# Splits without GpSimd, softmax sums under one reciprocal, and logits computed as rows, in a fused attention, mixture-of-experts and feed-forward kernel

## The chip, the cores and the metric

One core of one Trainium2 chip. The engines are TensorE (PE; its weight loads are shown as PEld), VectorE (DVE), ScalarE (ACT), GpSimd (POOL) and SyncE (SP, which here issues DMAs); each works through its own queue in order. The metric is the device time of one execution in microseconds.

## The reference

Attention over q, k, v of shape (4, 8, 576, 64) is a sum of two softmax attentions: one on rows averaged in fours (144 x 144 scores per head, the result repeated four times), and one on a band |i - j| < 4.

```python
out_up = np.repeat(sm_attn(q_d, k_d, v_d), 4, axis=2)       # q_d, k_d, v_d: means of four rows
scores = np.where(np.abs(pos[:, None] - pos[None, :]) < 4, scale * q @ k.T, -1e9)
x = (out_up + softmax(scores) @ v)                            # -> (2304, 512)
```

Then a mixture of 8 experts with a skip: only tokens with `x @ w_skip > 0` are computed, each by the expert with the largest logit, `x + p * (relu(x @ w1[e]) @ w2[e])`, with w1 (8, 512, 1024) and w2 (8, 1024, 512). Last a feed-forward: `h = x @ w_in` (512 to 2048), `g = h * sigmoid(1.702 h)`, `g @ w_out`.

## The kernel before

Matrix products of the experts and of the feed-forward run in float16 with split operands: a tensor t is scaled by a power of two, `high = f16(t)`, `low = f16(t - high)`, and three products (high high, high low, low high) are summed in PSUM. So each operand needs a maximum or a sum of squares (for the power of two), a high part and a low part. `pow2_into` and `pow2_scale` make the powers on DVE from exponent bits.

**Attention (`phase_a`)**: 16 units of two heads. Each step is a small function with a due time in `STAGE_A`; steps of all units are sorted by unit number plus due time and issued in that order; only SP's queue is then tied to that order, the rest is left to a scheduler that keeps it by priority. Of a unit: `ldq`, `ldv`, `ldw` load (SP), `qd`, `kd` sum rows in fours (DVE), `pd`, `pl`, `pk` are the scores (PE), `md` the maxima of the averaged scores and their scaling (DVE, L375, L376), `ed` the exponentials with their sums (ACT, L383), `mk`, `ml`, `sb`, `el` the same for the band, `rl` (L407 to L409) and `rd` (L414, L415) the reciprocals of the sums, `nl`, `nd` the products with them (POOL), `pq`, `pp` transposes, `pdt`, `pt` copies (ACT), `po`, `pn`, `pm` the products with v, `xt` the sum of both (DVE), `xm` its absolute maximum (DVE, L499), `px`, `xn` transpose and store. After every second unit `lg` (L530) forms 9 logits (8 experts and skip) for 576 tokens with the 9 logits on partitions; `le` (L539, L541) adds them up, and once per batch `tl` (L547) transposes them to tokens on partitions and `la` (L552) copies them for the routing (`route0` and on). PSUM has three double buffers (`big`) and two single ones (`small`). Steps of `Win` prepare w_in beside it.

**Experts (`phase_b`)**: each expert has 192 slots. `STAGE_B` gives due times again, and here all engines' queues are tied to that order. For an expert: `gather`, `xprep` (PE transposes), `xh`, `xl` (split of x), `l1` in four parts (PE, into PSUM `ph`, four buffers), `l1e` (ACT, relu to float32 `ht`, two buffers, L820), `l1h` (DVE, cast to `hh`, L823), `l1l` (POOL, `hl = ht - hh`, L827), `l2` in four parts (PE, L839, L846), `yrow`, `ymx`, `yadd`, `scatter`. The next experts' weights are loaded (`load`), squared and summed (`bound`, ACT, L689), scaled (`scale`, `scb`) and split (`hi` on ACT, L715, or DVE, L717; `lo` on DVE, `wl`, L723).

**Feed-forward (`phase_c`)**: 6 blocks of 384 tokens; layer one of a block is 16 column tiles `f` of 12 matmuls each (L1097, PSUM `ph`, three buffers), layer two runs two blocks behind (L1117). After each tile: sigmoid on ACT (L1101), the product `sg = ph * gs * sg` on DVE (L1102), and one tile later, in `late`, the cast `gh` on ACT (L1089) and the low part `gl` (L1090), on POOL in blocks 0 to 2 and on DVE after. `Wout` prepares w_out beside the first 40 tiles: load, `w64a` (ACT), `w64l`, `w64f` (DVE, L130 to L132), square (ACT, L231), scale, `woh` (ACT), `wol` (DVE, L243).

Of the kernel before, what the change touches and what calls it, by code (L numbers as in the profile page):

```python
# [80 lines left out]
def pow2_scale(nc, pool, m, name, squared=False):
# [19 lines left out]
    l10=-2.8750, l1e0=-2.5414, l1h0=-2.1815, l1l0=-2.0258, l20=-1.6661, l11=-2.8473, l1e1=-2.5379, l1h1=-2.2714,  # L101
    l1l1=-1.8902, l21=-1.5453, l12=-2.1639, l1e2=-1.9897, l1h2=-1.8716, l1l2=-1.8041, l22=-1.3442, l13=-2.0520,
    l1e3=-1.8744, l1h3=-1.8562, l1l3=-1.7262, l23=-1.2374, scale=-2.2810, scb=-2.1764, bound00=-3.9127,
    hi00=-3.1600, lo00=-2.9149, load00=-2.9138, bound01=-3.5859, hi01=-2.6890, lo01=-2.5881, load01=-2.5870,
    bound10=-2.7781, hi10=-2.1111, lo10=-1.8915, load10=-1.8904, bound11=-2.5563,
    hi11=-1.7296, lo11=-1.6624, load11=-1.6613, gather=-4.7500, xprep=-3.9203, xh=-3.5055, xl=-2.9872,
    giv=-1.1000, yrow0=-1.0047, yrow1=-1.0040, ymx=-0.8644, yadd0=-0.6966, scatter0=-0.6711,
# [1171 lines left out]
```

## Time and profile before

| | us |
|---|---|
| median of 3 runs | 803.38 |
| lowest, highest | 798.86, 803.81 |
| the profiled execution | 801.5 |
| its span, first to last instruction | 799.7 |

The span begins with attention (to about 200 us), then the experts (to about 391 us), then the feed-forward. The profile gives busy time by engine: PE 694.6 us, DVE 478.1, ACT 394.0, POOL 297.7; the mean granted TensorE clock is 0.948 of full speed. A busy PE is modelled, as its matmuls are pipelined: it says that PE has work in flight, not that it is at its peak. The views used below are the table of busy time by stretch, the groups of instructions by line, the list of who waited for whom, one line's spread of durations, and instructions in order of time.

### The profile page before, as it was taken

What the parts mean: (1) busy time and instruction counts of PE and PEld (TensorE: products, weight loads), DVE (VectorE), ACT (ScalarE), POOL (GpSimd) and SP (SyncE); (2) the same over time, 40 slices, a digit from 0 to 9 for tenths busy, and PEclk for the clock granted to TensorE, in tenths of its full rate; (3) what the DMA queues carried; (4) which work ended last, traced back from release to release, by engine and by line L of the source; (5) the groups of instructions that cost most, each with busy time, mean ns of one, the idle gap of its engine ahead of it and who ended that gap; (6) DMA issues with size and microseconds to landing.
All of it is one profiled execution on the core that took longest, in us unless ns stands there. A gap on an engine that the chain in (4) does not pass through costs nothing.

```text
span 799.7 us, 15485 instructions
## 1 busy us (share of the span) xinstructions
PE 694.6 (87%) x6207; PEld 430.8 (54%) x6207; DVE 478.1 (60%) x909; ACT 394.0 (49%) x806; POOL 297.7 (37%) x294
## 2 busy tenths in 40 slices
PE   4478978878499899878499899999999999999997
PEld 3355655655376666655265555545545545544443
DVE  8889997996588888899468996204503511520000
ACT  1566665763687667763167876414413412421111
POOL 8555644650346999987334444300000000000000
PEclk9977997999599999999799999999999999999999
DMA  9956998617456666520344331001000000000000
GB/s 259 263 152 174 301 285 260 158 33 258 113 205 237 241 234 240 189 73 16 119 132 146 123 102 27 1 26 54 1 27 14 1 13 27 1 14 27 27 27 27
DMA packets 43007, 92.49 MB, mean 116 GB/s; under 512 B 10398, under 2 KB 24354, under 8 KB 38837
## 3 DMA queue, kind: packets, MB, share of 16 engines
q1 hardware_dynamic: 25908, 81.11, 31.6%
q10 hardware_dynamic: 14208, 4.87, 2.6%
q0 software_dynamic: 2816, 5.50, 2.4%
q8 instruction: 50, 0.82, 0.4%
q14 instruction: 25, 0.20, 0.1%
HBM read 79.55 MB, written 12.92 MB: 116 GB/s over the span
## 4 chain that ended last, share of the span: by engine, by line
PE 48%; DVE 19%; POOL 11%; issue 9%; DMA 8%; ACT 4%; SPq 1%; POOLq 0%; ACTq 0%; DVEq 0%
PE po L1117 22%; PE ph L1097 17%; DMA w64r<-in_moe_w_in 5%; POOL hl L827 3%; DVE wl L723 3%; POOL g L881 3%; DVE w64l L131 2%; POOL ids L911 2%; POOL g L768 2%; DVE sg L1102 2%; DVE w64f L132 1%; DVE wol L243 1%; PE po L464 1%; DVE w64l L130 1%; DMA vw<-in_vwin 1%
## 5 line engine op out<-in xcount | busy, mean ns | idle before, releaser
L1102 DVE SCALAR_TENSOR_TENSOR sg<-ph,gs,sg 128x384 f32<-128x384 f32 x96 | 58.7, 615 | 132.3 <-ACT sg L1101 132.1
L1097 PEld LDWEIGHTS <-wih 128*128 128x128 f16 x768 | 76.2, 100 | 60.1 <-issue 12.4
L1123 ACT ACTIVATE o<-po,os 128x128 f32<-128x128 f32 x72 | 20.5, 367 | 148.8 <-PE po L1117 93.4
L1117 PEld LDWEIGHTS <-gh 128*128 128x128 f16 x576 | 56.3, 98 | 66.0
L1097 PE MATMUL ph<-xh,wih 128*128 128x384 f16 x384 | 79.5, 330 | 8.4 <-DVE sg L1102 7.5
L723 DVE SCALAR_TENSOR_TENSOR wl<-raw,w_s,wh 128x2048 f16<-128x2048 f32 x32 | 81.3, 2574 | 4.4 <-ACT wh L715 2.9
L1097 PE MATMUL ph<-xh,wil 128*128 128x384 f16 x384 | 79.9, 330 | 0.0
L1090 POOL TENSOR_TENSOR gl<-sg,gh 128x384 f16<-128x384 f32 x48 | 49.2, 1027 | 81.7 <-ACT gh L1089 63.2
L1097 PE MATMUL ph<-xl,wih 128*128 128x384 f16 x384 | 78.9, 328 | 0.0
L1089 ACT CAST gh<-sg 128x384 f16<-128x384 f32 x96 | 48.8, 509 | 47.8 <-DVE sg L1102 47.6
L1101 ACT ACTIVATE sg<-ph,ih 128x384 f32<-128x384 f32 x96 | 55.4, 578 | 33.2 <-PE ph L1097 31.1
L1117 PE MATMUL po<-woh,gh 128*128 128x512 f16 x288 | 67.1, 379 | 0.0
L689 ACT ACTIVATE jk<-raw 128x2048 f16<-128x2048 f32 x32 | 61.1, 1908 | 9.3 <-DVE mx L686 8.7
L1117 PE MATMUL po<-wol,gh 128*128 128x512 f16 x288 | 65.3, 379 | 0.0
L1117 PE MATMUL po<-woh,gl 128*128 128x512 f16 x288 | 65.1, 379 | 0.0
L827 POOL TENSOR_TENSOR hl<-ht,hh 128x384 f16<-128x384 f32 x32 | 43.5, 1372 | 27.2 <-DVE hh L823 17.4
L1097 PEld LDWEIGHTS <-wil 128*128 128x128 f16 x384 | 38.0, 99 | 25.5 <-issue 1.2
L812 PEld LDWEIGHTS <-wh 128*128 128x128 f16 x512 | 44.1, 101 | 4.4 <-ACT wh L715 2.3
L1117 PEld LDWEIGHTS <-gl 128*128 128x128 f16 x288 | 28.2, 98 | 34.0
L715 ACT ACTIVATE wh<-raw,w_s 128x2048 f16<-128x2048 f32 x16 | 31.3, 1995 | 29.6 <-DVE w_s L77 18.2
L1090 DVE TENSOR_TENSOR gl<-sg,gh 128x384 f16<-128x384 f32 x48 | 26.8, 558 | 26.5 <-ACT gh L1089 26.5
L812 PE MATMUL ph<-xh,wl 128*128 128x192 f16 x256 | 32.7, 252 | 3.9 <-DVE wl L723 3.6
(228 smaller groups left out, 1343.5 us busy)
## 6 DMA issues: line engine op xcount, KB each, us to landing
raw<-in_moe_w SPq DMA_DIRECT2D x32, 1024.0 KB
w64r<-in_moe_w_in SPq DMA_DIRECT2D x16, 512.0 KB
w64r<-in_moe_w_out SPq DMA_DIRECT2D x16, 512.0 KB
vw<-in_vwin SPq DMA_DIRECT2D x32, 216.0 KB
qt<-in_q SPq DMA_DIRECT2D x16, 288.0 KB
kt<-in_k SPq DMA_DIRECT2D x16, 288.0 KB
vn<-in_v SPq DMA_DIRECT2D x16, 288.0 KB
xd<-xn ACTq DMA_DIRECT2D x16, 288.0 KB
```

Of the source, the lines that this page charges most:

```text
L689: self.nc.scalar.activation(j, r, AF.Square, accum_out=self.mx[i][:, hf, wi:wi + 1])
L715: self.nc.scalar.activation(t, r, AF.Copy, scale=s)
L723: self.nc.vector.scalar_tensor_tensor(t, r, s, self.h[e, wi, hf], op0=ALU.mult, op1=ALU.subtract)
L812: T.matmul(ph[:, fi, :], wa[:, k_, o:o + P], xa[:, k_, :], start=(n == 0), stop=(n == 3 * NK - 1))
L827: G.tensor_tensor(hl[:, 2 * fp:2 * fp + 2, :], hr.pop((e, fp)), hh[:, 2 * fp:2 * fp + 2, :], ALU.subtract)
L881: G.tensor_tensor(g, g, yr[e][:, cols(ti)].rearrange("p (h w) -> p h w", w=DM // 2), ALU.add)
L1089: A.copy(split[1], split[0])
L1090: (nc.gpsimd if b <= ahead else V).tensor_tensor(split[2], split[0], split[1], ALU.subtract)
L1097: T.matmul(ph, wa[:, k_, f * P:(f + 1) * P], xx[:, k_, :], start=(n == 0), stop=(n == 3 * NK - 1))
L1101: A.activation(sg, ph, AF.Sigmoid, scale=ih[:, f:f + 1])
L1102: V.scalar_tensor_tensor(sg, ph, gs[:, f:f + 1], sg, op0=ALU.mult, op1=ALU.mult)
L1117: T.matmul(po, ga[:, f, i * P:(i + 1) * P], wa[:, f, :], start=(n == 0), stop=(n == 3 * (DF // P) - 1))
```

## The change

In attention `md` no longer scales; the scaling is a small ACT copy in `ed`. The sums of both softmaxes lie in one tile (13 columns, three tiles in turn), so `rl` takes one reciprocal for both and `rd` goes; the factor 4 that `rd` had goes into the copy `pdt`. `xm` is a sum of squares on ACT, and the scale of x comes from a bound by it. `lg` takes x as the stationary operand and the 9 gate columns as the moving one, so that logits come out with tokens on partitions; `tl` and `la` go. For the experts `l1e` goes: ACT writes `hh` from PSUM, and DVE computes `hl` from PSUM with a max and a subtraction; the due times of the old `l1e` and `l1h` are now those of `l1h` and `l1l`. In the feed-forward one gelu activation replaces sigmoid and product; `gh` and `gl` take the scale.

```diff
@@ pow2_into, pow2_scale: a target exponent t instead of 15 @@
+XT, WT = 3, 8
...
@@ STAGE_B @@
-    l10=-2.8750, l1e0=-2.5414, l1h0=-2.1815, l1l0=-2.0258, l20=-1.6661, ...
+    l10=-2.8750, l1h0=-2.5414, l1l0=-2.1815, l20=-1.6661, ...
...
@@ phase_a @@
+    sums = [cst.tile([P, NTL + 4], F32, name=f"sums{i}") for i in range(3)]
...
     def md(u):
-        V.tensor_scalar(m, m, -0.125 / 16.0, None, op0=ALU.mult)
...
     def ed(u):
-        d["rd"] = r = sm.tile([NPL, 4], F32, tag="rd", name="rd")
+        r = sums[u % 3][:NPL, NTL:NTL + 4]
+        mb = sm.tile([NPL, 4], F32, tag="mb", name="mb")
+        A.activation(mb, d["md"], AF.Copy, scale=-0.125 / 16.0)
...
     def rl(u):
-        d["rl"] = r = sm.tile([P, NTL], F32, tag="rl", name="rl")
-        V.tensor_reduce(r, d["sl"], axis=AX.X, op=ALU.add)
+        r = sums[u % 3]
+        V.tensor_reduce(r[:, 0:NTL], d["sl"], axis=AX.X, op=ALU.add)
         V.tensor_scalar(r, r, 1.0e-9, None, op0=ALU.add)
         V.reciprocal(r, r)
-    def rd(u):
-        r = units[u]["rd"]
-        V.tensor_scalar(r, r, 1.0e-9, 4.0, op0=ALU.add, op1=ALU.mult)
-        V.reciprocal(r, r)
...
     def pdt(u):
-        A.copy(o, d["pq"][:NPL, :, 0:4 * NPL])
+        A.activation(o, d["pq"][:NPL, :, 0:4 * NPL], AF.Copy, scale=0.25)
...
     def xm(u):
-        V.tensor_reduce(c["xm"][:, u:u + 1], units[u]["xt"], axis=AX.X, op=ALU.max, apply_absolute_value=True)
+        j = wk.tile([P, S], F16, tag="xj", name="xj", bufs=1)
+        A.activation(j, units[u]["xt"], AF.Square, accum_out=c["xm"][:, u:u + 1])
...
     def lg(u):
-        o = units[u]["lg"] = big("lg")
-        for a in range(2):
+        o = units[u]["lg"] = small("lg")
+        for j in range(NTB):
             for i in range(2):
-                T.matmul(o[:9, a, 0:S // 2], wg9[:, units[u - 1 + i]["pr"], :],
-                         units[u - 1 + i]["xt"][:, a * S // 2:(a + 1) * S // 2], start=(i == 0), stop=(i == 1))
+                T.matmul(o[:TB, 9 * j:9 * j + 9], units[u - 1 + i]["xt"][:, TB * j:TB * (j + 1)],
+                         wg9[:, units[u - 1 + i]["pr"], :], start=(i == 0), stop=(i == 1))
...
     def le(u):
-        src = d["lg"][:9, :, 0:S // 2]
+        src = d["lg"][:TB, 0:9 * NTB].rearrange("p (j e) -> p j e", j=NTB)
...
-    def tl(b):
...
-    def la(b):
...
@@ Experts.scale2: one operation less for iv @@
...
@@ phase_b @@
-    V.tensor_copy(c["xmax"], mp)
-    sx, ix = pow2_scale(nc, c["cp"], c["xmax"], "sx")
+    sx, ix = pow2_scale(nc, c["cp"], mp, "sx", True, t=XT)
+    V.tensor_scalar(c["xmax"], ix, 2.0 ** XT, None, op0=ALU.mult)
...
-    def l1e(e, fp):
-        ph, (hh, hl) = phs.pop((e, fp)), hts[e]
-        hr[e, fp] = t = wk.tile([P, 2, CAP], F32, tag="ht", name="ht")
-        A.activation(t, ph, AF.Relu, scale=C20)
     def l1h(e, fp):
-        V.tensor_copy(hts[e][0][:, 2 * fp:2 * fp + 2, :], hr[e, fp])
+        A.activation(hts[e][0][:, 2 * fp:2 * fp + 2, :], phs[e, fp], AF.Relu)
     def l1l(e, fp):
-        hh, hl = hts[e]
-        G.tensor_tensor(hl[:, 2 * fp:2 * fp + 2, :], hr.pop((e, fp)), hh[:, 2 * fp:2 * fp + 2, :], ALU.subtract)
+        hh, hl = (h[:, 2 * fp:2 * fp + 2, :] for h in hts[e])
+        V.scalar_tensor_tensor(hl, phs.pop((e, fp)), 0.0, hh, op0=ALU.max, op1=ALU.subtract)
...
@@ phase_c @@
-    gs = sm.tile([P, NF], F32, name="gs")
-    V.tensor_scalar(gs, win.si, smin, C20, op0=ALU.mult, op1=ALU.mult)
+    gs = sm.tile([P, 1], F32, name="gs")
+    V.tensor_scalar(gs, sx, smin, C20, op0=ALU.mult, op1=ALU.mult)
...
         def late():
             if split:
-                A.copy(split[1], split[0])
-                (nc.gpsimd if b <= ahead else V).tensor_tensor(split[2], split[0], split[1], ALU.subtract)
+                A.activation(split[1], split[0], AF.Copy, scale=gs)
+                V.scalar_tensor_tensor(split[2], split[0], gs, split[1], op0=ALU.mult, op1=ALU.subtract)
...
-            A.activation(sg, ph, AF.Sigmoid, scale=ih[:, f:f + 1])
-            V.scalar_tensor_tensor(sg, ph, gs[:, f:f + 1], sg, op0=ALU.mult, op1=ALU.mult)
+            A.activation(sg, ph, AF.Gelu_apprx_sigmoid, scale=ih[:, f:f + 1])
```

## Rows read from the trace of the kernel before

**Rows 1.** Busy us (x instructions) of PE, PEld, DVE, ACT, POOL; PE clock, DMA share, GB/s.

```profile
40.00:120.00 80.00, 64.27 (x1086) 46.69 (x1084) 73.79 (x181) 51.56 (x156) 42.96 (x47) 0.85 0.79 228
...
240.00:340.00 100.00, 90.88 (x893) 65.87 (x890) 88.34 (x109) 70.79 (x80) 85.34 (x60) 0.98 0.65 228
...
400.00:480.00 80.00, 73.22 (x458) 45.92 (x457) 68.72 (x114) 59.49 (x126) 32.32 (x30) 0.98 0.38 125
480.00:800.00 320.00, 314.36 (x1650) 162.34 (x1649) 78.09 (x137) 99.26 (x218) 16.84 (x18) 0.99 0.06 20
```

**Rows 2.** DVE by line, 0 to 200: busy us, mean ns | idle before, releaser.

```profile
L499 DVE TENSOR_REDUCE xm<-xt 128x1 f32<-128x576 f32 x16 | 11.8, 738 | 0.1
...
L414 DVE TENSOR_SCALAR rd<-rd 72x4 f32<-72x4 f32 x16 | 5.8, 365 | 4.0 <-ACT sd L383 3.1 <-POOL vd L328 0.8
...
L376 DVE TENSOR_SCALAR md<-md 72x4 f32<-72x4 f32 x16 | 3.1, 192 | 0.0
...
L541 DVE TENSOR_TENSOR le<-le,lg 9x576 f32<-9x576 f32 x4 | 2.9, 737 | 0.9 <-PE lg L530 0.9
...
L415 DVE RECIPROCAL rd<-rd 72x4 f32<-72x4 f32 x16 | 2.6, 161 | 0.1
```

**Rows 3.** PE in order of time, end of attention: start, us, line, records.

```profile
184.81 2.11 PE L530 MATMUL lg<-xt,wg 128*9 128x288 f32 x8
...
187.63 1.27 PE L464 MATMUL po<-pt,vw 128*64 128x64 f32 x36
...
193.60 0.45 PE L547 MATMUL tl<-ident,le 9*96 9x9 f32 x6
```

**Rows 4.** ACT by line, 0 to 200: a square with a sum.

```profile
L181 ACT ACTIVATE w64j<-w64f 128x512 f16<-128x512 f32 x16 | 10.0, 628 | 8.2 <-DVE w64f L132 6.8 <-DVE md L376 0.9 <-DVE rd L415 0.4
...
L181 ACT ACTIVATION_READ_ACCUMULATOR w64j<-w64f 128x1 f32 x16 | 3.0, 188 | 0.0
```

**Rows 5.** SP's DMA issues in order of time: two band windows, eight units apart.

```profile
51.37 0.84 SPq L320 DMA_DIRECT2D vw<-in_vwin  x2
...
131.53 1.04 SPq L320 DMA_DIRECT2D vw<-in_vwin  x2
```

**Rows 6.** Experts, 240 to 340: cast and subtraction by line, the cast's min/median/max.

```profile
L823 DVE CAST hh<-ht 128x384 f16<-128x384 f32 x20 | 11.8, 611 | 10.1 <-ACT ht L820 10.1
...
L827 POOL TENSOR_TENSOR hl<-ht,hh 128x384 f16<-128x384 f32 x21 | 31.6, 1513 | 6.8 <-DVE hh L823 6.6
...
L823 DVE CAST hh<-ht x20: 346/396/1420, 242.2 to 338.1; 128x384 f16<-128x384 f32 x20
```

**Rows 7.** Who waited for whom, 190 to 400: us, times, longest.

```profile
PE py L839 <- DVE wl L723: 15.4, 7, 4.3
...
ACT ht L820 <- POOL hl L827: 13.8, 5, 3.2
```

**Rows 8.** PE in order of time: layer two begins for experts 1, 2, 6.

```profile
253.87 0.59 PE L839 MATMUL py<-wh,hh 128*128 128x512 f16 x2
...
272.32 0.59 PE L839 MATMUL py<-wh,hh 128*128 128x512 f16 x2
...
358.72 0.59 PE L839 MATMUL py<-wh,hh 128*128 128x512 f16 x2
```

**Rows 9.** Feed-forward: a wait (399 to 481), min/median/max of lines, groups by line.

```profile
PE ph L1097 <- DVE sg L1102: 7.5, 8, 2.2
...
L1102 DVE SCALAR_TENSOR_TENSOR sg<-ph,gs,sg x96: 601/618/620, 406.4 to 707.1; 128x384 f32<-128x384 f32 x96
...
L1101 ACT ACTIVATE sg<-ph,ih x96: 560/580/592, 405.8 to 706.5; 128x384 f32<-128x384 f32 x96
...
L1089 ACT CAST gh<-sg x96: 493/511/529, 407.1 to 707.8; 128x384 f16<-128x384 f32 x96
...
L243 DVE SCALAR_TENSOR_TENSOR wol<-w64f,wo_s,woh 128x512 f16<-128x512 f32 x11 | 12.0, 1102 | 0.0
...
L243 DVE SCALAR_TENSOR_TENSOR wol<-w64f,wo_s,woh x16: 740/752/1404, 436.3 to 498.5; 128x512 f16<-128x512 f32 x16
...
L1101 ACT ACT_TABLE_LOAD x1 | 1.3, 1283 | 0.0
```

More of the change, by code (lines that the diff above doesn't have):

```diff
@@ L76, in pow2_into, with pow2_scale @@
     V.tensor_scalar(e, e, 64.0 * ONE, 200.0 * ONE, op0=ALU.max, op1=ALU.min)
-    V.tensor_scalar(s.bitcast(I32), e, -1.0, 268.0 * ONE, op0=ALU.mult, op1=ALU.add)
-    V.tensor_scalar(si.bitcast(I32), e, 14.0 * ONE, None, op0=ALU.subtract)
-def pow2_scale(nc, pool, m, name, squared=False):
+    V.tensor_scalar(s.bitcast(I32), e, -1.0, (253.0 + t) * ONE, op0=ALU.mult, op1=ALU.add)
+    V.tensor_scalar(si.bitcast(I32), e, (t - 1.0) * ONE, None, op0=ALU.subtract)
+def pow2_scale(nc, pool, m, name, squared=False, t=15):
     e = pool.tile([P, 1], I32, name=f"{name}_e")
@@ L100 @@
 STAGE_B = dict(
[L101 to L107, printed above, removed]
+    l10=-2.8750, l1h0=-2.5414, l1l0=-2.1815, l20=-1.6661, l11=-2.8473, l1h1=-2.5379, l1l1=-2.2714, l21=-1.5453,
+    l12=-2.1639, l1h2=-1.9897, l1l2=-1.8716, l22=-1.3442, l13=-2.0520, l1h3=-1.8744, l1l3=-1.8562, l23=-1.2374,
+    scale=-2.2810, scb=-2.1764, bound00=-3.9127, hi00=-3.1600, lo00=-2.9149, load00=-2.9138, bound01=-3.5859,
+    hi01=-2.6890, lo01=-2.5881, load01=-2.5870, bound10=-2.7781, hi10=-2.1111, lo10=-1.8915, load10=-1.8904,
+    bound11=-2.5563, hi11=-1.7296, lo11=-1.6624, load11=-1.6613, gather=-4.7500, xprep=-3.9203, xh=-3.5055,
+    xl=-2.9872, giv=-1.1000, yrow0=-1.0047, yrow1=-1.0040, ymx=-0.8644, yadd0=-0.6966, scatter0=-0.6711,
     yadd1=-0.6113, scatter1=-0.6009, scat0=-2.8208, scat1=-2.5500, scat2=-1.6433)
@@ L294, in phase_a @@
     vws = [cst.tile([P, NTL, 2, D], F32, name=f"vw{i}") for i in range(4)]
+    sums = [cst.tile([P, NTL + 4], F32, name=f"sums{i}") for i in range(3)]
+    for t in sums:
+        V.memset(t, 1.0)
     for t in vws:
@@ L418, in nd @@
         d = units[u]
[L419 removed]
+        G.tensor_tensor(d["sd"], d["sd"], sums[u % 3][:NPL, NTL:NTL + 4, None].to_broadcast([NPL, 4, 2 * NPL]), ALU.mult)
     def nl(u):
         d = units[u]
[L423 removed]
+        G.tensor_tensor(d["sl"], d["sl"], sums[u % 3][:, 0:NTL, None].to_broadcast([P, NTL, KW]), ALU.mult)
     def pq(u):
@@ L535, in le @@
         r = rt[d["b"]]
-        src = d["lg"][:9, :, 0:S // 2]
+        src = d["lg"][:TB, 0:9 * NTB].rearrange("p (j e) -> p j e", j=NTB)
         if d["pr"] == 1:
-            r["le"] = sm.tile([9, 2, S // 2], F32, tag="le", name="le", bufs=2)
-            V.tensor_copy(r["le"], src)
-        else:
-            V.tensor_tensor(r["le"], r["le"], src, ALU.add)
-    def tl(b):
-        rt[b]["tl"] = o = small("tl")
-        le = rt[b]["le"].rearrange("e a t -> e (a t)")
-        for j in range(NTB):
-            T.transpose(o[:TB, 9 * j:9 * j + 9], le[:, TB * j:TB * (j + 1)], ident[:9, :9])
-    def la(b):
-        r = rt[b]
-        r["l"] = sm.tile([TB, NTB, 9], F32, tag="l", name="l", bufs=2)
-        V.tensor_copy(r["l"], r["tl"][:TB, 0:9 * NTB].rearrange("p (j e) -> p j e", j=NTB))
+            r["l"] = sm.tile([TB, NTB, 9], F32, tag="l", name="l", bufs=2)
+            V.tensor_copy(r["l"], src)
+        else:
+            V.tensor_tensor(r["l"], r["l"], src, ALU.add)
     def tmp(nm, shape, dt=F32):
@@ L646, in phase_a @@
     for u in range(NU):
-        for fn in (ldq, ldw, ldv, vd, qd, kd, pl, pk, pd, mk, ml, sb, el, rl, nl, md, ed, rd, nd, pq, pp,
+        for fn in (ldq, ldw, ldv, vd, qd, kd, pl, pk, pd, mk, ml, sb, el, rl, nl, md, ed, nd, pq, pp,
                    pdt, pt, po, pn, pm, od, xt, xm, px, xn):
@@ L655, in phase_a @@
         if u % NPR == NPR - 1:
-            for fn in (tl, la, route0, rk, route1, eq, ohv, sel, sacc, slots, count, gate):
+            for fn in (route0, rk, route1, eq, ohv, sel, sacc, slots, count, gate):
                 sched.append((u + STAGE_A[fn.__name__], len(sched), fn, (u // NPR,)))
@@ L928, in phase_b @@
     for i in range(NK):
-        for fn in (l1, l1e, l1h, l1l, l2):
+        for fn in (l1, l1h, l1l, l2):
             fns[f"{fn.__name__}{i}"] = lambda e, fn=fn, i=i: fn(e, i)
```

18 lines of the change are left out of this document (7 added, 11 removed).

## The prediction

> **What bounds the kernel now.** I read the busy time by stretch first, because the three stages have different limits. In the attention stage (first row of [rows 1]) VectorE (DVE) works 73.8 of 80 us, the 16 DMA engines are busy 0.79 of the time and TensorE (PE) 64 of 80 us at a granted clock of 0.85: DVE leads, but two others are close behind. In the experts' stage (second row of [rows 1]) DVE 88, POOL 85 and PE 91 of 100 us: three engines that wait for each other. In the first fifth of the last stage (third row of [rows 1]) PE has 73 and DVE 69 of 80 us; behind it (fourth row of [rows 1]) PE has 314 of 320 us and everything else is cover. So time can be won in the first 480 us only; from there on DVE and ACT work is free either way.
>
> Next I read who waits for whom. In the experts' stage ACT's relu waits 13.8 us for POOL's subtraction `hl` (it needs the buffer `ht` back), and PE waits 15.4 us for DVE's `wl` [rows 7]. The `hl` subtractions are 31.6 of POOL's 85 us [rows 6]. The first matmuls of layer two of experts 1, 2 and 6 start at 253.87, 272.32 and 358.72 [rows 8]: 104.85 us for five experts, 20.97 each, but 18.45 for the one period in which PE did not wait. That is the gap to be won.
>
> **The change part by part: attention (16 units).** DVE loses `xm` (16 x 0.738 = 11.8 us), the scaling of the maxima (3.1), the two small operations of `rd` (5.8 and 2.6) [rows 2]. Of the eight passes over the logits at 9 partitions, 0.737 us each [rows 2], eight passes over 54 columns at 96 partitions stay; I price one at 0.2 us, between nothing and the 0.37 us of the four-column `rd` [rows 2], and book 8 x 0.54 = 4.3 us. The copy `la` goes as well; I leave it out. Sum: 27.6 us, 1.7 us a unit. The reciprocal over 13 columns instead of 9 costs nothing I can see: it waits for nothing new, since `ed` lies 1.7 units ahead of `rl`, and POOL's `nd` came right behind `nl`, which waited for `rl` already.
>
> ACT takes this over: a Square with sum over 576 columns. The same form over 512 columns takes 0.628 and its accumulator read 0.188 us [rows 4], so 0.70 + 0.19, and a four-column Copy that the trace does not show; I take 0.2 us, near the accumulator read, between nothing and 0.63. 16 x 1.1 = 17 us, on an engine that has 28 of 80 us free [rows 1]. The square has xt behind it for a whole unit by its due time, so it holds up nothing behind it on ACT; the Copy stands ahead of the exponentials on ACT in place of a DVE operation ahead of them, a wash.
>
> On PE a logits step was 8 records of 288 columns, 2.11 us [rows 3]. Now it is 12 products in fp32, so 24 records by the same doubling, each with weights of 96 columns and 9 columns moved. The nearest rows are 36 such records with 64 columns in 1.27 us, 35 ns each, and a bound above is 75 ns, what the six transposes from 9 partitions take (6 in 0.45 us) [rows 3]: 0.85 to 1.8 us. I take 1.2, as the form is nearer the first. The six transposes go. But the logits tile moves from the three large PSUM buffers to the two small ones, where the band scores, the counts and the sums wait too: a PE that waits there for DVE to read is new, and DVE is the engine that is late.
>
> What is it worth? Units pass at (131.53 - 51.37) / 8 = 10.0 us [rows 5]. With DVE 1.7 us lighter its own limit falls from 9.2 to 7.5 us; but the DMA engines need 0.79 x 10 = 7.9 and PE 8.0 us, and all are in-order queues that feed each other. Floor: a gain of 2 us a unit over some ten units in steady state, 20 us; nothing, if PE's waits and its clock (0.85 here, so it already falls to its lower level of 1.2 GHz at times) eat it. Between these I take 0.75 us a unit for the ten, 7.5, and 1.5 us at the end of the stage, where logits, transposes, copy and routing follow each other with nothing beside them: **-9 us (0 to -20)**.
>
> **The experts' stage.** POOL loses `hl`, so its 85 us become 54 of 100. ACT writes `hh` straight from PSUM, as long as the relu it replaces. DVE loses the cast (0.611 us mean) and gets max-and-subtract from PSUM; the nearest form is the gate product from PSUM over the same 128x384, 0.618 us [rows 6, 9]. DVE's sum stays, 88 us of 100 [rows 1], but the cast is stretched: its median is 0.396 [rows 6]. If that stretch came with POOL's work and the new form has none, nothing is won or lost; if the cast would have been 0.396 anyway, 4 x 0.22 = 0.9 us a period is lost. On the other side DVE's 11.7 us of idle time per 100 [rows 1] is mostly waiting for ACT's relu, which waited for POOL, and that goes: 20.97 x 0.883 = 18.5 us is DVE's new floor, and 18.45 PE's [rows 8]. Two engines at the same floor do not both reach it; I take 19.2, a gain of 1.8 us over six periods: **-11 us (0 to -16)**, the ends being 21 us and 18.45 us a period, with a microsecond more at the tail. The scale of x costs two more small DVE operations and one less copy ahead of the first gather: +0.3 us, an estimate from the four-column operations [rows 2]. One operation less in the experts' inverse scales and the other exponents lie beside `wl`, which DVE has to do anyway; uncovered they would be tenths of a microsecond. The factor 0.25 in the copy `pdt` leaves it one ACT pass.
>
> Of the wait that this adds: PSUM's `ph` (four buffers) now comes free when DVE has subtracted, not when ACT has copied. The second half of an expert's layer one on PE needs the buffer of its first half; DVE's `l1l0` is due 0.13 of a period, 2.7 us, ahead of it. While DVE keeps its due times nothing waits; if it is 2.7 us late, PE stands, and behind it on PE the next expert.
>
> **The last stage.** ACT: the gelu takes the sigmoid's place, 0.580 us median; the copy `gh` now has a scale read from memory, as the sigmoid has, so 0.511 becomes at most 0.58 [rows 9], 32 x 0.07 = 2.2 us over the 80 us, of ACT's 20 us of slack [rows 1]. DVE: max one pass over 128x384 before (0.618) and after; no gain in count. But POOL leaves: `wol` takes 1.102 us on average here and 0.752 in the median [rows 9], 11 x 0.35 = 3.9 us, beside POOL's `gl`, and PE's buffer is free after the gelu, no longer after the DVE product behind it. PE's wait for that product is 7.5 us [rows 9]; that, and nothing below, bounds the gain: **-5 us (0 to -7.5)**, since ACT, at 59 + 2 of 80 us, has to keep a faster pace too. From 480 us on DVE gets a pass less in half of the blocks; hidden behind PE, as the fourth row of [rows 1] has it.
>
> The Trainium skill (SBUF — State Buffer, on the port pair that VectorE and GpSimd share) says that a DVE operation with two SBUF inputs and a GpSimd operation that reads SBUF exclude each other for the whole instruction, while one SBUF input beside PSUM excludes nobody. The trace agrees with the first half: `wol` reads two SBUF tiles and has a maximum of 1.404 against a median of 0.752. By that rule the new subtraction from PSUM is never stretched, which leaves my sum as it is.
>
> **Sum.** The profiled execution took 801.5 us (span 799.7); -9 - 11 + 0.3 - 5 = -24.7 gives 776.8. The median of the runs shown is 803.4, 1.9 us above the profiled one. I say **777 us**.
>
> **The rivals.** *Gains stay hidden.* DVE is late on `l1l`, so the new PSUM wait replaces the old one, and attention stays at the pace of DMA and PE. For it: three engines within 10% of each other in both stages. Against it: one period did run in 18.45 us. Price: attention -2, experts -4, last stage -2: 793.
>
> *More is won.* Attention follows DVE to its floor (-20), the experts PE to theirs (-16), and all of 7.5 at the end: 801.5 - 43 = 758. Against it: no stretch of attention shows DMA and DVE full together.
>
> *Tables are reloaded: slower.* In the last stage, squares for w_out's scales alternate with the activation. If the gelu's table lacks Square, each of 16 squares costs two table loads of 1.283 us [rows 9]: 41 us on ACT. ACT has some 20 us free of 80 there [rows 1], so the stretch grows by about 21 us and its gain of 5 goes, against 20 won before: near 803 at the least, and up to 801.5 - 20 + 41 = 822 if the loads stand ahead of what PE waits for; the middle is 812. It decides from some 31 loads on (20 us of slack and 20 us of gain, at 1.283). Against it: Square and Sigmoid shared a table here, with one load in the stage [rows 9]. The Trainium skill (ScalarE: Activation LUTs, on table sets) says that cheap functions such as relu, copy, identity and abs are in every set; it does not name Square there, and no run so far shows the gelu's set.
>
> **How the numbers follow.** My forecast, anything from 764 to 788: 0.62. Hidden gains, 788 to 803: 0.17. More won, 750 to 764: 0.14. Slower by tables or by logits that hold up PE: 0.07. A measurement of this kernel tells about 1% (8 us) from no change. Faster by over 1% (under 795.3): 0.62 + 0.14 + a third of 0.17 = 0.82; within 1%: 0.11; slower: 0.07. To leave out no more than 2 in 10, the range goes from 760, inside the larger gain, to 796, the half of the hidden case.
>
> **What would show it.** Right: attention's last logits some 9 us earlier; no wait of ACT for POOL in the experts' stage, first matmuls of layer two some 19 us apart; `wol` and the integer joins of w_out near their medians, PE's wait for `sg` gone, one table load in the last stage. Wrong: PE waiting for the DVE subtraction `hl`, a DMA share above 0.9 in attention with no shorter stage, PE waiting for small PSUM buffers, or a granted clock in attention under 0.85 because PE has more idle time.

## The result and the profile after

The changed kernel took 781.6 us in the median (781.45 to 782.92, four runs), the kernel before 801.54 (798.86 to 803.81, four runs): ratio 0.9756, 95% interval 0.9717 to 0.9795. The profiled execution has a span of 779.8 us against 799.7. Forecast were 777 and a range of 760 to 796, so the total lies 4.6 us from the forecast. The terms that it was summed from do not lie so near:

| stage, by the trace | before | after | change | forecast (bounds) |
|---|---|---|---|---|
| attention: start to the last routing sum (`sa`) | 200.0 | 212.3 | +12.3 | -9 (0 to -20) |
| up to the first layer-two matmul of the experts | 33.9 | 34.3 | +0.4 | +0.3 |
| from there to the first matmul of the feed-forward | 165.8 | 144.6 | -21.2 | -11 (0 to -16) |
| from there to the end of the span | 400.0 | 388.6 | -11.4 | -5 (0 to -7.5) |

Attention went the wrong way, the other two stages won about twice what was forecast, and the errors cancelled: that the total came out near is luck. The same four stretches as in [rows 1], from the changed kernel's busy time by stretch (busy us and instructions of PE, PEld, DVE, ACT, POOL; granted TensorE clock, DMA share, GB/s):

```profile
40.00:120.00 80.00, 68.49 (x1157) 55.38 (x1158) 67.71 (x154) 61.53 (x192) 44.19 (x50) 0.87 0.83 237
240.00:340.00 100.00, 98.97 (x992) 73.05 (x992) 94.73 (x114) 86.02 (x98) 69.03 (x40) 1.00 0.74 251
400.00:480.00 80.00, 80.00 (x518) 51.09 (x517) 66.60 (x137) 74.48 (x150) 0.00 (x0) 1.00 0.38 122
480.00:779.80 299.80, 295.45 (x1543) 151.01 (x1541) 38.60 (x62) 89.82 (x189) 0.00 (x0) 1.00 0.05 19
```

In the experts' stage PE is now busy for 99 of 100 us (91 before), in the feed-forward's first 80 us for all of them (73 before). In attention DVE is relieved (67.7 instead of 73.8 of 80 us), but nothing came of it. Later stretches of attention show why, by the same view of the changed kernel and, in the second fence, of the kernel before:

```profile
120.00:160.00 40.00, 33.46 (x530) 27.48 (x528) 28.17 (x74) 24.50 (x71) 15.39 (x20) 0.66 0.69 198
160.00:200.00 40.00, 34.10 (x515) 28.28 (x514) 23.03 (x66) 22.58 (x64) 12.77 (x17) 0.74 0.22 61
```

```profile
120.00:160.00 40.00, 34.94 (x653) 24.79 (x651) 34.51 (x94) 24.45 (x72) 22.20 (x24) 0.88 0.78 209
160.00:200.00 40.00, 30.93 (x477) 22.88 (x477) 31.20 (x99) 20.96 (x53) 12.00 (x16) 0.98 0.45 146
```

PE is busy for about as long as before, DVE for less, and PE's granted clock is 0.66 and 0.74 instead of 0.88 and 0.98.

Experts and feed-forward, from the instructions in order of time (layer two of experts 1 and 6 begins), the groups by line (240 to 340) and the spread of single lines of the changed kernel:

```profile
264.53 0.59 PE L822 MATMUL py<-wh,hh 128*128 128x512 f16 x2
...
353.17 0.59 PE L822 MATMUL py<-wh,hh 128*128 128x512 f16 x2
```

```profile
L810 DVE SCALAR_TENSOR_TENSOR hl<-ph,hh 128x384 f16<-128x384 f32 x22 | 11.6, 547 | 0.0
L806 ACT ACTIVATE hh<-ph 128x384 f16<-128x384 f32 x23 | 10.5, 479 | 0.0
...
L243 DVE SCALAR_TENSOR_TENSOR wol<-w64f,wo_s,woh x16: 743/746/754, 423.3 to 475.2; 128x512 f16<-128x512 f32 x16
...
L1073 DVE SCALAR_TENSOR_TENSOR gl<-sg,gs,gh x96: 608/619/621, 398.0 to 683.5; 128x384 f16<-128x384 f32 x96
...
L1084 ACT ACTIVATE sg<-ph,ih x96: 556/580/588, 396.8 to 682.2; 128x384 f32<-128x384 f32 x96
...
L1072 ACT ACTIVATE gh<-sg,gs x96: 598/614/624, 397.4 to 682.9; 128x384 f16<-128x384 f32 x96
...
PE ph L1080 <- ACT xh L1059: 0.8, 1, 0.8
```

An expert takes (353.17 - 264.53) / 5 = 17.73 us. `wol` is not stretched any more, 743 to 754 ns where [rows 9] had 740 to 1404. In the experts' stage, where POOL still works 69 of 100 us, `wl` still is at times (at most 2.83 us against a median of 2.35; before, 3.72). The last row is all that PE waits for in layer one and two of the feed-forward; the 7.5 us of [rows 9] are gone.

### The profile page after: what moved, and what is told of

The parts are those of the page before. It is cut to its first block, busy times and chain, and to the rows that moved or that the text cites. A ratio compares the mean times of both kernels' runs of the same rounds, so it can differ in the third digit from the quotient of the medians.

```text
span 779.8 us, 15482 instructions
## 1 busy us (share of the span) xinstructions
PE 697.7 (89%) x6311; PEld 452.0 (58%) x6311; DVE 402.5 (52%) x790; ACT 416.4 (53%) x854; POOL 213.0 (27%) x214
## 4 chain that ended last, share of the span: by engine, by line
PE 68%; DMA 11%; issue 5%; DVE 5%; ACT 4%; POOL 4%; SPq 1%; ACTq 0%; POOLq 0%; DVEq 0%
PE ph L1080 24%; PE po L1099 23%; PE ph L800 6%; DMA w64r<-in_moe_w_in 4%; PE py L822 3%; PE py L829 2%; PE pp L441 2%; PE po L463 2%; DMA xd<-xn 2%; DMA vw<-in_vwin 1%; DMA xd<-gt 1%; DMA xd<-g,idu 1%; POOL ids L894 1%; ACT jk L679 1%; PE px L1057 1%
## 5 line engine op out<-in xcount | busy, mean ns | idle before, releaser
L1073 DVE SCALAR_TENSOR_TENSOR gl<-sg,gs,gh 128x384 f16<-128x384 f32 x96 | 59.1, 617 | 180.7 <-ACT gh L1072 180.4
L711 DVE SCALAR_TENSOR_TENSOR wl<-raw,w_s,wh 128x2048 f16<-128x2048 f32 x32 | 76.3, 2422 | 7.4 <-ACT wh L703 7.3
L1099 PE MATMUL po<-woh,gh 128*128 128x512 f16 x288 | 65.1, 379 | 0.0
L1072 ACT ACTIVATE gh<-sg,gs 128x384 f16<-128x384 f32 x96 | 58.8, 613 | 2.5
L1080 PEld LDWEIGHTS <-wil 128*128 128x128 f16 x384 | 37.8, 98 | 25.2 <-issue 0.7
L363 PE MATMUL pl<-kt,qt 64*32 64x38 f32 x1152 | 22.2, 232 | 19.4 <-DMA kt<-in_k 14.5
L441 PE MATMUL pp<-ident,sl 128*38 128x128 f32 x128 | 24.3, 354 | 16.5 <-ACT pdt L447 9.6
L864 POOL TENSOR_TENSOR g<-g,yr 128x512 f32<-128x512 f32 (+1 forms) x14 | 31.8, 2272 | 24.2 <-ACT yr L848 24.0
L126 ACT ACTIVATE w64a<-w64r 128x512 f32<-128x512 f32 x32 | 21.3, 666 | 30.1 <-DMA w64r<-in_moe_w_in 28.9
```

The costliest lines, as they stand in the source:

```text
L441: T.transpose(dst, d["sl"][:, t, :], ident)
L711: self.nc.vector.scalar_tensor_tensor(t, r, s, self.h[e, wi, hf], op0=ALU.mult, op1=ALU.subtract)
L864: G.tensor_tensor(g, g, yr[e][:, cols(ti)].rearrange("p (h w) -> p h w", w=DM // 2), ALU.add)
L1072: A.activation(split[1], split[0], AF.Copy, scale=gs)
L1073: V.scalar_tensor_tensor(split[2], split[0], gs, split[1], op0=ALU.mult, op1=ALU.subtract)
L1080: T.matmul(ph, wa[:, k_, f * P:(f + 1) * P], xx[:, k_, :], start=(n == 0), stop=(n == 3 * NK - 1))
```

## Experiments: which part of the change did what

Each of the first four kernels has one stage as before and the rest as changed, or the reverse; the fifth adds work to the feed-forward. The stage ends (last routing sum, first layer two of experts, first matmul of the feed-forward, end of span) are those of the one profiled execution of each kernel and tell where the time went. Ratios are to the kernel before. Where `xm` is the absolute maximum again, the scale of x is made from it with another target exponent and the same number of instructions (the same holds for the later kernels with the old `xm`).

**All of attention as before, the rest changed.**

```diff
-        A.activation(mb, d["md"], AF.Copy, scale=-0.125 / 16.0)
+        V.tensor_scalar(m, m, -0.125 / 16.0, None, op0=ALU.mult)        # and rd, as before
-        A.activation(j, units[u]["xt"], AF.Square, accum_out=c["xm"][:, u:u + 1])
+        V.tensor_reduce(c["xm"][:, u:u + 1], units[u]["xt"], axis=AX.X, op=ALU.max, ...)
-        o = units[u]["lg"] = small("lg")                                # and lg, le, tl, la as before
+        o = units[u]["lg"] = big("lg")
```

> The changed kernel with the whole attention stage of before (maxima scaled and both reciprocals on DVE, xm as an absolute maximum on DVE, logits at 9 partitions with their transposes); experts and feed-forward as changed. The scale of x is made from the absolute maximum with another target exponent, which changes no instruction count. Theory A (attention itself got 12 us slower, and the other two stages won 21 and 11 us): 781.6 - 12 = 769 to 770 us, the last routing sum near 200 us instead of 212. Rival (the three stages push each other, for instance by when the experts' first weights land): the gain of the experts' stage shrinks as attention ends earlier, total 776 to 782.

Measured: 769.54 us (766.89 to 770.91), ratio 0.9564 (0.9505 to 0.9623); stage ends 200.3, 233.2, 377.0, 766.7.

**Attention as changed, the rest as before.**

```diff
-        V.tensor_reduce(c["xm"][:, u:u + 1], ...)        # experts and feed-forward untouched
+        A.activation(j, units[u]["xt"], AF.Square, accum_out=c["xm"][:, u:u + 1])
```

> The kernel before with the changed attention alone (the scale of x by the sum of squares, target exponent of before); experts and feed-forward of before. If attention itself lost: 801.5 + 12 = 812 to 815 us, last routing sum near 212 us. If the loss in the changed kernel belongs to that one order of work only and not to the attention edits: 798 to 806.

Measured: 816.6 us (812.82 to 819.76), ratio 1.0141 (1.008 to 1.0202); stage ends 218.0, 251.8, 418.3, 817.9. Both directions agree that the changed attention alone loses: 12.1 us of the median in the first run, 1.4% (0.8 to 2.0, some 6 to 16 us) here. The profiled execution here has the last sum 18.0 us later than the kernel before.

**The experts' split as before**, with the due times that go with it.

```diff
-        A.activation(hts[e][0][:, 2 * fp:2 * fp + 2, :], phs[e, fp], AF.Relu)
+        V.tensor_copy(hts[e][0][:, 2 * fp:2 * fp + 2, :], hr[e, fp])
-        V.scalar_tensor_tensor(hl, phs.pop((e, fp)), 0.0, hh, op0=ALU.max, op1=ALU.subtract)
+        G.tensor_tensor(hl[:, 2 * fp:2 * fp + 2, :], hr.pop((e, fp)), hh[...], ALU.subtract)
```

> The changed kernel with the experts' split of before (relu to float32 on ACT, cast on DVE, subtraction on POOL). If POOL's subtraction was the cause of the experts' 20.9 us a period: a period of 20.5 to 21 us again, 17 to 21 us more, total 799 to 803, ACT waiting some 14 us for POOL. Rival (the period fell because of fewer small DVE operations and other due times): less than 8 us more, total under 790.

Measured: 803.46 us (796.99 to 806.28), ratio 0.9976 (0.9944 to 1.0008); stage ends 215.4, 249.1, 414.5, 803.4. The experts' stage is back at 165.4 us. Its waits (us, times, longest) and one stretch of busy time are near those of the kernel before again:

```profile
ACT ht L809 <- POOL hl L816: 13.2, 5, 2.7
PE py L828 <- DVE wl L712: 12.2, 5, 4.3
...
260.00:360.00 100.00, 87.17 (x847) 62.81 (x845) 87.09 (x100) 74.84 (x85) 85.55 (x59) 0.98 0.61 215
```

The rival with fewer small DVE operations falls, as these stay here. What the due times alone are worth was not tried.

**The feed-forward as before.**

```diff
-                A.activation(split[1], split[0], AF.Copy, scale=gs)
+                A.copy(split[1], split[0])
+                (nc.gpsimd if b <= ahead else V).tensor_tensor(split[2], split[0], split[1], ALU.subtract)
-            A.activation(sg, ph, AF.Gelu_apprx_sigmoid, scale=ih[:, f:f + 1])
+            A.activation(sg, ph, AF.Sigmoid, scale=ih[:, f:f + 1])
+            V.scalar_tensor_tensor(sg, ph, gs[:, f:f + 1], sg, op0=ALU.mult, op1=ALU.mult)
```

> The changed kernel with the feed-forward of before (sigmoid, product on DVE, cast, subtraction on POOL in blocks 0 to 2 and on DVE after). If all 11.4 us of that stage came from this edit: total 792 to 794. If part of it came from an earlier or better placed start: 785 to 790.

Measured: 788.76 us (785.26 to 790.95), ratio 0.9809 (0.9755 to 0.9863); stage ends 209.7, 242.9, 386.5, 786.0: the feed-forward takes 399.5 us, as before.

**GpSimd beside the new feed-forward.** The new code stays; in blocks 0 to 2 POOL forms a useless difference that nobody reads.

```diff
+                if b <= ahead:
+                    nc.gpsimd.tensor_tensor(pj, split[0], split[1], ALU.subtract)
```

> The changed kernel with a useless POOL subtraction of the same shape as the old gl (sg minus gh, 128x384, into a tile that nobody reads) beside each tile of feed-forward blocks 0 to 2. Theory L (lock: POOL's reads stretch DVE operations with two SBUF inputs): the mean of wol goes from 746 ns to about 1100 and the new gl, which reads two SBUF tiles, from 619 to 900 or more; total 785 to 793. Theory P (what was won is that PE's buffer comes free after the gelu and no longer after the DVE product): no change, 780 to 784, although wol is stretched.

Measured: 787.54 us (785.72 to 793.56), ratio 0.9807 (0.9742 to 0.9871); stage ends 209.5, 243.5, 388.4, 787.1. The feed-forward takes 398.7 us: one instruction per tile that nobody waits for takes 10.1 of the stage's 11.4 us away. Groups by line and two waits, 388 to 480:

```profile
L1076 POOL TENSOR_TENSOR pj<-sg,gh 128x384 f16<-128x384 f32 x35 | 39.7, 1134 | 63.0 <-ACT gh L1072 62.4
L1073 DVE SCALAR_TENSOR_TENSOR gl<-sg,gs,gh 128x384 f16<-128x384 f32 x35 | 30.1, 868 | 9.3 <-ACT gh L1072 9.3
...
L243 DVE SCALAR_TENSOR_TENSOR wol<-w64f,wo_s,woh 128x512 f16<-128x512 f32 x14 | 13.0, 926 | 0.2 <-ACT woh L242 0.2
...
ACT w64j L231 <- DVE w64f L132: 11.9, 10, 2.1
PE ph L1083 <- ACT sg L1087: 5.8, 8, 1.7
```

`gl` goes from 0.619 to 0.868 us and `wol` from 0.746 to 0.926, and PE waits again, 5.8 us, now for the gelu. The way there can be read too: ACT's square of w_out (`w64j`) waits 11.9 us for DVE's `w64f`, and the gelu stands in the same queue; the changed kernel has no such wait. PE's buffer is free after the gelu here, as in the changed kernel, so the earlier release of the buffer did not win the stage by itself; POOL had to leave. Whether POOL's leaving would have won as much without the earlier release, no run shows. The Trainium skill (SBUF — State Buffer, two separate sides) says that GpSimd and a DVE operation with two SBUF inputs lock each other out of their shared ports; both stretched rows are DVE operations with two SBUF inputs, so the trace agrees.

## Experiments: what attention lost

The five kernels here undo parts of the changed attention, one or two at a time.

**Only the logits as before** (`lg`, `le`, `tl`, `la`).

```diff
-        o = units[u]["lg"] = small("lg")
-        for j in range(NTB):
+        o = units[u]["lg"] = big("lg")
+        for a in range(2):
```

> The changed kernel with the logits of before alone (288 columns moved per product, 9 partitions, transposes, copy; large PSUM buffers). Theory C (clock: the short logits left PE idle more often, its granted clock fell to 0.66 to 0.74 between 120 and 200 us, and half-speed PE sets the pace): granted clock there back to 0.88 or more, attention ends 8 to 12 us earlier, total 770 to 774. Theory Q (ACT's queue: the square of xm and the copy mb stand on ACT between DVE and PE): no gain, the longer logits cost 2 to 6 us more, total 781 to 788.

Measured: 762.81 us (759.84 to 764.24), ratio 0.9468 (0.9411 to 0.9526), the fastest of all kernels here; last routing sum at 194.7.

**Only `xm` as before**, on DVE.

```diff
-        A.activation(j, units[u]["xt"], AF.Square, accum_out=c["xm"][:, u:u + 1])
+        V.tensor_reduce(c["xm"][:, u:u + 1], units[u]["xt"], axis=AX.X, op=ALU.max, ...)
```

> The changed kernel with xm as the absolute maximum on DVE again (scale of x from it, other target exponent). Theory Q: ACT no longer waits 7.5 us for xt ahead of the square and the copies, exponentials and transposes behind it come earlier: attention ends 6 to 12 us earlier, total 770 to 776. Theory C: PE's idle time is not changed by this, total 779 to 784.

Measured: 796.7 us (793.98 to 798.87), ratio 0.9891 (0.983 to 0.9952); last sum at 229.9. The theory that the square blocks ACT's queue and so delays PE is contradicted: with the square gone the stage is 17.6 us longer. From 50 us to the last sum PE is busy for 146.1 us and idle for 33.8, where the changed kernel has 137.1 and 25.2, and the granted clock in 120 to 160 is 0.63. Why the clock is lower still with `xm` on DVE is not settled.

**Only the softmax part as before** (scaling of the maxima, two reciprocals).

```diff
-        A.activation(mb, d["md"], AF.Copy, scale=-0.125 / 16.0)
+        V.tensor_scalar(m, m, -0.125 / 16.0, None, op0=ALU.mult)
+    def rd(u):
+        V.tensor_scalar(r, r, 1.0e-9, 4.0, op0=ALU.add, op1=ALU.mult)
+        V.reciprocal(r, r)
```

> The changed kernel with the two softmaxes' small operations of before (maxima scaled on DVE, two reciprocals, factor 4 in the second). Theory Q in its other half (the copy mb on ACT ahead of the exponentials, and the band's reciprocal bound to the exponentials of the averaged scores): attention ends 3 to 8 us earlier, total 774 to 779. Theory C, or Q by the square alone: within 3 us of 781.6, with 11 us more work on DVE.

Measured: 780.15 us (774.84 to 785.59), ratio 0.9674 (0.961 to 0.9738): not to be told from the changed kernel by its median. (Its profiled execution was the slowest of the four, 785.6 us, with the last sum at 218.9.)

**With the old logits, `xm` or the softmax part as before too.** The first has logits and `xm` of before (softmax new), the second logits and softmax of before (`xm` on ACT).

```diff
-        A.activation(j, units[u]["xt"], AF.Square, accum_out=c["xm"][:, u:u + 1])      # the first
+        V.tensor_reduce(c["xm"][:, u:u + 1], units[u]["xt"], axis=AX.X, op=ALU.max, ...)
-        A.activation(mb, d["md"], AF.Copy, scale=-0.125 / 16.0)                        # the second
+        V.tensor_scalar(m, m, -0.125 / 16.0, None, op0=ALU.mult)
```

> The changed kernel with the logits and the absolute maximum xm of before; the softmax part (scaling of the maxima on ACT, one reciprocal) stays new. The scale of x is made from a maximum again, with another target exponent and the same number of instructions as before. With the old logits throughout, all of attention as before gave 769.5 (last routing sum 200.3), and new softmax and new xm together gave 762.8 (194.7). If those 6 us come from xm leaving DVE, this gives 768 to 771 with the last sum at 199 to 201; if they come from the softmax part, 761 to 765 with the last sum at 194 to 196; if from both, 765 to 768. By the busy time taken off DVE (xm 11.8 us, softmax 11.5 us) both theories stand equal, so I expect the middle.

> The changed kernel with the logits and the softmax part of before (scaling of the maxima and two reciprocals on DVE); only xm stays on ACT as a sum of squares. The counterpart of the run before it. If the 6 us between 769.5 and 762.8 come from xm leaving DVE, this gives 761 to 765 with the last routing sum at 194 to 196; if from the softmax part, 768 to 771 with the sum at 199 to 201; if from both, 765 to 768.

Measured: 773.72 us (769.4 to 780.06), ratio 0.9639 (0.9551 to 0.9727), last sum at 201.6; and 763.87 us (761.95 to 770.72), ratio 0.953 (0.9453 to 0.9608), last sum at 194.2. With the old logits the four combinations make a square:

| old logits; last routing sum, median | softmax old | softmax new |
|---|---|---|
| `xm` on DVE | 200.3, 769.5 | 201.6, 773.7 |
| `xm` on ACT | 194.2, 763.9 | 194.7, 762.8 |

`xm` on ACT is worth some 6 us of the stage, the softmax part nothing, though each took about the same busy time off DVE (11.8 and 11.5 us). The new logits then cost 212.3 - 194.7 = 17.6 us.

## Experiments: why the new logits cost 17.6 us

**Large PSUM buffers for the new logits**, as the old ones had.

```diff
-        o = units[u]["lg"] = small("lg")
+        o = units[u]["lg"] = big("lg")[:, 0, :]
```

> The changed kernel with one line edited: the tile of the logits lies in the three large PSUM buffers again, as before the change; the products stay the new ones, with 9 columns moved. Two theories of why the new logits cost attention some 17 us. Small-buffer theory: the tile now shares the two small PSUM buffers with the band scores, the counts and the sums, and PE waits there for DVE. Then this edit gives back most of it: the last routing sum at 195 to 201 (new logits in small buffers: 212.3; old logits: 194.7), the granted clock in 120 to 160 up from 0.66 to 0.84 or more, the median 762 to 768. Clock theory: 9 columns moved instead of 288 leave PE with less to do, the granted clock falls to the lower level for longer, and which buffer takes the result is indifferent. Then the last sum stays at 208 to 220, the clock in 120 to 160 at 0.62 to 0.75, the median 778 to 790. A share of both would lie between, 769 to 777.

Measured: 788.92 us (782.65 to 792.3), ratio 0.9797 (0.9712 to 0.9882); last sum at 220.2. Nothing came back, so the small-buffer theory falls.

**More work for PE.** The new logits stay, and the old products are formed as well, for nothing.

```diff
+        o = big("lf")
+        for a in range(2):
+            for i in range(2):
+                T.matmul(o[:9, a, 0:S // 2], wg9[:, units[u - 1 + i]["pr"], :],
+                         units[u - 1 + i]["xt"][:, a * S // 2:(a + 1) * S // 2], ...)
```

> The changed kernel plus useless work on PE: ahead of each of the eight steps of new logits, the four old products of 288 columns are formed too, into a large PSUM tile that nobody reads. Nothing is taken away. Clock theory: PE does some 16 us more work in all and still gains, because the granted clock in 120 to 160 comes back from 0.66 to 0.84 or more: the last routing sum at 195 to 203 instead of 212.3, the median 764 to 772. Any theory in which the new logits cost by waits, by the small buffers, by the order of the steps or by their own length: the filler is added on top, the last sum at 213 to 230, the median 782 to 798, with the clock in 120 to 160 under 0.8.

Measured: 776.97 us (774.29 to 780.9), ratio 0.9654 (0.9583 to 0.9724); last sum at 212.5. The stretches of attention in these two, the large buffers first, then the kernel with the useless products, then that with the old logits:

```profile
120.00:160.00 40.00, 32.18 (x541) 25.68 (x541) 28.50 (x67) 25.17 (x78) 15.89 (x20) 0.71 0.73 212
160.00:200.00 40.00, 36.00 (x532) 29.92 (x530) 25.71 (x72) 24.25 (x67) 18.72 (x21) 0.65 0.20 47
```

```profile
120.00:160.00 40.00, 36.04 (x683) 28.86 (x683) 31.69 (x81) 28.21 (x86) 19.61 (x24) 0.87 0.86 241
160.00:200.00 40.00, 39.61 (x602) 30.95 (x603) 26.35 (x75) 26.39 (x72) 16.33 (x19) 0.91 0.41 129
```

```profile
120.00:160.00 40.00, 35.13 (x614) 26.34 (x613) 35.81 (x89) 29.88 (x91) 26.23 (x26) 0.87 0.77 217
160.00:200.00 40.00, 31.25 (x443) 23.00 (x441) 26.50 (x96) 21.32 (x54) 10.08 (x14) 0.88 0.51 160
```

Half of the clock theory's forecast came true. The clock did come back, from 0.66 and 0.74 to 0.87 and 0.91. The end of the stage did not move, 212.5 against 212.3: PE is now busy for 39.6 of 40 us in 160 to 200, with eight steps of useless products, 2.11 us each at the higher level [rows 3], some 17 us.

How much of the 17.6 us is the clock's can be read from PE's time between 50 us and the last sum. Same view; the kernel before, the changed one, the one with the old logits, the one with the useless products:

```profile
50.00:200.00 150.00, 123.06 (x2128) 89.01 (x2126) 130.52 (x350) 90.68 (x259) 73.07 (x81) 0.90 0.73 212
50.00:212.30 162.30, 137.09 (x2226) 113.19 (x2226) 114.26 (x297) 103.98 (x304) 67.89 (x82) 0.78 0.67 196
50.00:194.70 144.70, 122.03 (x2122) 89.79 (x2122) 117.73 (x299) 103.14 (x304) 75.41 (x81) 0.90 0.76 219
50.00:212.50 162.50, 145.28 (x2291) 110.50 (x2290) 115.85 (x298) 104.09 (x305) 71.61 (x83) 0.86 0.69 200
```

Between the old logits and the new, PE is busy for 15.1 us longer (122.0 to 137.1) and idle for 2.5 us longer (22.7 to 25.2): it hardly waits more, its work takes longer. A mean clock of 0.78 says that 0.44 of the stretch ran at the lower level, 0.90 that 0.20 did, some 71 and 29 us. If PE is busy there as in the mean and its work takes twice as long (the products `po` below take 1.17 us there and 0.66 at the higher level), that costs 30 and 12 us, an estimate of 18 us more with the new logits, enough for the 15.1. With the useless products PE is busy for 8.2 us longer than in the changed kernel and idle for 8.0 us less (17.2), so of their some 17 us about half filled idle time and about half is what the higher clock gave back. The other kernels with the changed attention fit: from 50 us to the last sum their clock is 0.80 where the stage ends at 209.5, 0.77 at 209.7, 0.76 at 215.4, and 0.74 at 218.0 and 220.2. A kernel with the new logits, a high clock and no useless work was not found.

Where the clock falls can be read in the changed kernel. PE in order of time, then three stretches of 2 us around it:

```profile
124.50 0.66 PE L480 MATMUL po<-pdt,vd 72*64 72x144 f32 x8
...
158.50 2.21 PE L531 MATMUL lg<-wg,xt 128*96 128x9 f32 x24
160.56 0.73 PE L431 MATMUL pq<-ident,sd 72*72 72x72 f32 x8
161.22 0.93 PE L463 MATMUL po<-pt,vw 128*64 128x64 f32 x20
...
163.32 1.17 PE L480 MATMUL po<-pdt,vd 72*64 72x144 f32 x8
```

```profile
158.00:160.00 2.00, 2.00 (x26) 1.81 (x24) 2.00 (x5) 1.95 (x5) 1.92 (x3) 1.00 0.58 147
160.00:162.00 2.00, 2.00 (x37) 1.88 (x36) 2.00 (x5) 0.53 (x2) 1.42 (x2) 0.94 0.03 8
162.00:164.00 2.00, 2.00 (x27) 1.70 (x25) 1.19 (x2) 2.00 (x11) 0.21 (x1) 0.50 0.00 0
```

The clock falls from 2.4 to 1.2 GHz just under 162 us, right behind a step of logits, with PE busy in every microsecond; the same eight products `po` then take 1.17 us instead of 0.66. The steps at 108.46 and 125.78 are followed by a fall in the same way; behind three later ones the clock holds for at least 3 us. The 3 us up to these two falls, and in the kernel with the old logits the 3 us up to a fall at 132.2:

```profile
107.60:110.60 3.00, 3.00 (x36) 2.63 (x35) 2.94 (x7) 2.68 (x8) 0.76 (x1) 0.99 1.03 296
124.60:127.60 3.00, 3.00 (x95) 2.75 (x90) 2.96 (x7) 2.76 (x8) 1.11 (x2) 1.00 0.87 211
129.20:132.20 3.00, 2.28 (x43) 1.79 (x43) 3.00 (x8) 2.06 (x6) 0.72 (x1) 0.99 1.04 324
```

The five kernels with the old logits show 23 falls between 50 us and the last sum, and the last row is the one with the busiest PE: in each it was idle for 0.7 us or more of the 3 us before. The nine with the new logits show falls behind idle time too, but also 23 with PE busy in all of the 3 us, each time with 14 to 24 records of new logits in them (one of the 23 in the kernel with the useless products, at 164.9 us). The kernel before has four old steps between 146 and 196 us and a granted clock of 1.00 throughout:

```profile
146.00:196.00 50.00, 42.13 (x745) 31.11 (x742) 42.49 (x131) 28.97 (x78) 20.81 (x24) 1.00 0.45 135
```

The busy share does not tell the steps apart; what they do does: 24 records (12 products) that move 9 columns behind weights of 96, against 8 records that move 288 behind weights of 9. And the new step saves no time even at the higher level, 2.21 us against 2.11. Its groups by line, 100 to 213, products and weight loads:

```profile
L531 PE MATMUL lg<-wg,xt 128*96 128x9 f32 x144 | 13.5, 231 | 0.0
...
L531 PEld LDWEIGHTS lg<-wg,xt 128*96 128x96 f32 x144 | 13.0, 167 | 0.7 <-issue 0.4 <-PE sel L599 0.2
```

Six steps, 13.5 us, of which weight loads run in 13.0: the step is as long as its weight loads, 13.0 / 144 = 90 ns each. At the lower level a step takes 4.01 us, 167 ns a record (the run with large buffers, at 112.19 us). The Trainium skill (TensorE: Matmul & The Clock Gate, LDWEIGHTS) has the load time go with the columns of the weight; by its formula 96 columns are an estimate of 80 ns and 64 of 53. The trace is near the first at the higher level alone, and not near the second: 36 records of `po` with 64 columns take 35 ns each [rows 3].

## Why the prediction was right or wrong, point by point

**Attention, -9 forecast, +12.3 measured: wrong, and outside its bounds.** DVE was relieved, by 20.6 us of the 27.6 booked (busy for 172.2 us up to the last sum before, 151.6 after). Two steps failed; the third doubt below came to nothing.

- The price of the logits on PE. "0.85 to 1.8 us. I take 1.2, as the form is nearer the first": measured 2.21. The one row has weights of 64 columns, the other 96 columns but on 9 partitions only, so neither bounded a weight of 96 columns on 128.
- The end of the range at "nothing, if PE's waits and its clock [...] eat it". Here the clock took more than the gain. A lower clock was named among the signs to look for, with "because PE has more idle time" as its reason. In the trace PE had no more idle time than before (25.2 us against 26.9 from 50 us to the last sum); its products had changed. "Logits that hold up PE" stood among the slower cases without a price, and the stage's range had no loss in it at all.
- "But the logits tile moves from the three large PSUM buffers to the two small ones": not priced in the sum, and it needed no price, as the run with large buffers shows.

The value for DVE's relief was not wrong in kind: with the old logits the stage ends at 194.7, 5.3 us earlier than before. The softmax part adds nothing to that; the prediction had given both the same worth per microsecond of DVE.

"The square has xt behind it for a whole unit by its due time, so it holds up nothing behind it on ACT": ACT does wait for `xt` at the square, 8.4 us in all, since only SP's queue is tied to the due times here. That wait did not decide: with `xm` on ACT the kernel is faster, with the old logits and with the new.

**Prologue, +0.3 forecast, +0.4 measured.**

**Experts, -11 forecast, -21.2 measured: right mechanism, wrong size, beyond the bound of -16.** ACT's wait for POOL is gone, PE is the bound, and the undoing run gives all of it back. The mis-sized terms: the 18.45 us taken as PE's floor, of which PE was busy for 18.2, were no floor, as a period now takes 17.73; and 19.2 was taken because "two engines at the same floor do not both reach it", but DVE's floor was not 18.5: 94.73 of 100 us at 17.73 us a period are 16.8 us an expert. `l1l` takes 0.547 us and not 0.618, and two small operations shrank by more than that: one step of the weights' exponents `w_e` from 0.768 to 0.170 us (0.769 again with the split as before), and `giv`, two an expert, from 0.445 to 0.152 (0.154 also with the split as before, so not by POOL's subtraction). From the first expert's layer two to the seventh's it is 106.5 us instead of 124.8, 18.3 of the 21.2; the rest is won behind it.

**Feed-forward, -5 forecast, -11.4 measured: right mechanism, beyond the bound of -7.5.** "PE's wait for that product is 7.5 us [rows 9]; that, and nothing below, bounds the gain" is the step that failed. The wait itself was sized rightly, but the stage won more than PE's idle time. From its first matmul to the end of the span, before and after:

```profile
399.70:799.70 400.00, 387.88 (x2108) 208.39 (x2107) 147.12 (x250) 159.06 (x344) 49.16 (x48) 0.99 0.12 41
391.20:779.80 388.60, 384.24 (x2108) 207.58 (x2107) 107.43 (x202) 168.74 (x344) 0.00 (x0) 1.00 0.13 42
```

PE's idle time fell by 7.8 us (12.12 to 4.36), nearly all of it that wait, and its busy time by 3.6. One piece of that can be read in the kernel before, PE in order of time and one stretch:

```profile
478.35 0.41 PE L1074 MATMUL px<-ident,x 128*128 128x128 f32 x2
480.97 1.07 PE L1097 MATMUL ph<-xh,wih 128*128 128x384 f16 x4 [2.21 <-DVE sg L1102]
481.84 1.49 PE L1097 MATMUL ph<-xh,wil 128*128 128x384 f16 x4
...
485.25 0.81 PE L1097 MATMUL ph<-xh,wil 128*128 128x384 f16 x4
...
480.00:490.00 10.00, 9.03 (x48) 5.36 (x48) 5.62 (x14) 7.09 (x15) 4.68 (x5) 0.83 0.10 26
```

Behind a wait of 2.21 us four matmuls take 1.49 instead of 0.81 us, and the clock of the next 10 us is 0.83: another 1.7 us. The remaining 2 us are not traced. Nor is that fall a rule: the kernel with the feed-forward as before has none behind its waits (granted clock 1.00 from 400 to 780 us), and its stage still takes 399.5 us with PE idle for 12.2. Of the two reasons given, POOL leaving and the earlier free buffer, the run with POOL beside the new code shows that the second alone does not win the stage.

**The rivals.** No table is reloaded: one load stands in the last stage, though 16 squares alternate with the gelu, so both are in one set here. PE's wait for the subtraction `hl` did not come; the buffer `ph` was free in time. The larger gain (758) was near in the two later stages and absent in the first: with the old logits the kernel takes 762.8 us, 38.7 less than before.

## What to carry to other kernels

Where a total comes out right, compare the stages before believing its terms. Taking GpSimd off beside DVE operations with two SBUF inputs was worth more than its own waits said, since DVE operations around it shrink and the waits of ACT and PE behind them go. A product with few columns moved behind wide weights was no saving on TensorE here: price it by the weight loads, and look at the granted clock of what follows it.
